# A Strassen step for a part of the second sequence product, with operand sums made beside the scores

## The chip, the cores and the metric

The kernel runs on one NeuronCore of a Trainium2 chip. The time is the device time of one execution in microseconds; a figure for a kernel is the median over its runs. A profile is one further execution, recorded by the hardware profiler. The engines are named as in the profile: PE is TensorE (matrix products), PEld its weight loads, DVE is VectorE, ACT is ScalarE, POOL is GpSimd, SP is SyncE, which here only issues transfers. ScalarE issues transfers too.

## The reference

With x of 2048 positions (S) by 640 features (D), the result is `g * a + (1 - g) * b`, where `g = sigmoid(sum(x * gate_w))` per position.

- Branch a is the real part of a two-dimensional Fourier transform by matrices: `a = Cr @ (x @ Dr.T) - Ci @ (x @ Di.T)`, with Cr and Ci of 2048 by 2048 (the first and second sequence matrix) and Dr and Di of 640 by 640.
- Branch b is a layer of 256 experts with product keys. Each position has 32 heads; each head scores two times 16 keys, takes the best two of each sixteen, adds them to four candidates, keeps the best two and weighs them by a softmax. A chosen expert e contributes `gelu(x . u[e]) * v[e]`.

All of it is in float32.

## The kernel before

**Order of branch a.** The kernel multiplies by the sequence matrices first and keeps the result in DRAM as `pd[w, c]`, with w the matrix (0 for Cr, 1 for Ci) and c one of four chunks of 512 positions. A chunk of a matrix is 16 **pieces** (w, c, s), each a 128x512 block loaded to a tile `wf`. `seq_piece` multiplies one piece by the five 128-wide tiles of x (d = 0 to 4) into five PSUM banks that gather the 16 pieces of a chunk. There are 128 pieces, in the order w, c, s. The **last part** (`step`) multiplies by the 640 by 640 matrices; it is already a Strassen form, in two halves b of 42 steps each, seven units of six steps (a11, a12, s1, s2, s4, s3, a22).

**Products.** A float32 operand is split into a high part (ScalarE, `split`, L123) and a low part (L124, POOL or VectorE). `mm3` makes a product of three matmuls from them (L128 to L130). Pieces are loaded five ahead and split three ahead, into a ring `WS` of four.

**Branch b runs between the pieces.** Work is hung on piece numbers with `at(n, f)` and emitted by `follow(n)` after piece n. Pieces 0 to 30 are beside the preparation of the score weights. Pieces 31 to 70 are the **score stage**: for each of eight pairs p of 128-position tiles, five pieces and four `score_half` calls (five products each), then `u_pair`. ScalarE copies scores from two alternating banks (5 and 6) to tiles `sc`, of which there are two; VectorE takes the top two of each sixteen from them (`topk`), and every four tiles `gates` computes the weights, with one exponential on ScalarE. `rows` then transposes the results by transfers and copies them. After that follows the **expert work** (`experts`): 32 builds of 0/1 matrices on VectorE into four hot buffers (L579 to L581, three operations each), their matmuls (`use`, L607, 32 small ones per build), a copy out of PSUM by ScalarE (L588), and a store to `gd`. Two hot buffers are given up before the last part (L932, L933), because their room becomes a part of the ring there.

**What sets the order.** Each engine executes its instructions in the order in which the program emits them. VectorE work of branch b is emitted by a credit account (`Pump`): each product of TensorE calls `run_bg(0.68)`, which earns 0.68 times a share; while the account is positive, the next piece of work is emitted and its booked price taken off (for a build 3.3, for a `use` 0.2). With nothing to emit, the account is set to 0. Other VectorE work takes its price off the account too (`bg.credit -= ...`). The share is 0.95 before the expert work opens, 1.25 after, 0.95 for the last eight pieces, and in the last part 0.0 for ten steps and then 1.05 (L921, L941). The expert work opens when all 16 tiles' rows are there (L923 and following), which needs p2's pool to be closed. `load_z(b, n)` loads, for the last part, sums of the expert work of half b; before that it emits all expert work still needed for that half (`bg.drain`, L772). For the second half this is hung on step 38 of the first (L914).

**Queues.** SP issues nearly all loads, in order; an issue that must wait for a buffer or for data holds up all behind it. ScalarE issues the stores.

## Time and profile before

| | us |
|---|---|
| median of 3 runs | 773.94 (773.1 to 774.1) |
| the profiled execution's own time | 773.85 |
| its span, first to last instruction | 772.1 |
| TensorE busy | 766.7 |
| VectorE busy | 516.2 |
| POOL busy | 346.5 |
| ScalarE busy | 287.3 |

The span is what the profile's rows divide; the rest of the execution's own time, 1.75 us, lies around it. Matmuls are pipelined, so a row's duration for one is longer than the distance from one to the next. A group's row gives the line, engine, operation, output and inputs, shapes and count, then the busy time and mean of one in ns, then the engine's idle time ahead of the group and what ended it. Rows of one tile or line give the minimum, median and maximum in ns, and the first and last start. Rows of a timeline give the start, the duration and the instruction. Rows of stretches give, for each engine, its busy time and count.

### The profile page before, as it was taken

How to read it: one execution, taken by the hardware profiler on the slowest of the kernel's cores; microseconds unless marked ns; L12 is line 12 of the kernel's file. 1: busy time of each engine (PE TensorE's matmuls, PEld its weight loads, DVE VectorE, ACT ScalarE, POOL GpSimd, SP SyncE). 2: the span in 40 equal slices, each digit the busy share in tenths (PEclk: the TensorE clock that was granted, in tenths of full speed). 3: DMA queues.
4: the chain of work that ended last, by engine and by line, in shares of the span. 5: the costliest groups of instructions: out<-in, count | busy, mean ns of one | idle time of the engine just before them, and what ended most of it. 6: DMA issues, size and time to landing. Idle time of an engine off the chain costs nothing.

```text
span 772.1 us, 11964 instructions
## 1 busy us (share of the span) xinstructions
PE 766.7 (99%) x4616; PEld 620.3 (80%) x4616; DVE 516.2 (67%) x611; ACT 287.3 (37%) x470; POOL 346.5 (45%) x235
## 2 busy tenths in 40 slices
PE   9999999999999999999999999999999999999997
PEld 6777677888888888888888888777788888788886
DVE  7642122276888698579988592677677789747761
ACT  5334324322214432353343462332243453543341
POOL 4522224315143242325242875343446765577253
PEclk9999999999999999999999999999999999999999
DMA  9976985603030440223325454453565586686411
GB/s 343 375 259 191 315 317 191 213 0 117 14 102 25 149 147 15 84 67 130 120 54 169 138 157 122 97 153 89 143 187 169 184 296 218 204 252 220 128 54 70
DMA packets 86953, 121.21 MB, mean 157 GB/s; under 512 B 33136, under 2 KB 40432, under 8 KB 86896
## 3 DMA queue, kind: packets, MB, share of 16 engines
q1 hardware_dynamic: 57360, 100.64, 39.7%
q10 hardware_dynamic: 29536, 19.81, 8.1%
q8 instruction: 36, 0.59, 0.3%
q14 instruction: 21, 0.17, 0.1%
HBM read 98.91 MB, written 19.93 MB: 154 GB/s over the span
## 4 chain that ended last, share of the span: by engine, by line
PE 98%; ACT 1%; POOL 0%; issue 0%; DVE 0%; ACTq 0%; DVEq 0%
PE b L128 31%; PE b L129 31%; PE b L130 31%; PE b L326 2%; PE b L607 1%; PE b L338 1%; PE b L211 1%; PE b L278 0%; POOL WS L124 0%; ACT L396 0%; ACT WS L123 0%; ACT ST L806 0%; ACT wp L332 0%; ACT WP L123 0%; ACT ST L218 0%
## 5 line engine op out<-in xcount | busy, mean ns | idle before, releaser
L124 POOL TENSOR_TENSOR WS<-wf,WS 128x512 fp32r<-128x512 f32 x126 | 189.6, 1509 | 279.3 <-ACT WS L123 250.3
L128 PE MATMUL b<-WS,X 128*128 128x512 f32 x635 | 251.2, 396 | 0.2 <-ACT ST L218 0.2
L129 PE MATMUL b<-WS,X 128*128 128x512 f32 x635 | 247.6, 390 | 0.0
L130 PE MATMUL b<-WS,X 128*128 128x512 f32 x635 | 247.5, 390 | 0.0
L128 PEld LDWEIGHTS b<-WS,X 128*128 128x128 f32 x635 | 119.2, 188 | 33.4 <-issue 7.3
L130 PEld LDWEIGHTS b<-WS,X 128*128 128x128 f32 x635 | 119.2, 188 | 25.4
L129 PEld LDWEIGHTS b<-WS,X 128*128 128x128 f32 x635 | 119.3, 188 | 23.5
L123 ACT ACTIVATE WS<-wf 128x512 fp32r<-128x512 f32 x128 | 80.6, 630 | 113.7 <-PE b L130 57.2
L443 DVE TENSOR_REDUCE mm<-sc 128x64 f32<-128x1024 f32 x32 | 39.0, 1219 | 46.3 <-ACT sc L429 45.7
L124 POOL TENSOR_TENSOR xl<-xf,xh 128x640 fp32r<-128x640 f32 x16 | 33.6, 2123 | 70.4 <-ACT xh L123 64.0
L124 POOL TENSOR_TENSOR WS<-ra,WS 128x512 fp32r<-128x512 f32 x40 | 59.7, 1512 | 12.0 <-ACT WS L123 12.0
L130 PE MATMUL b<-WU,xl 128*128 128x512 f32 x160 | 62.2, 389 | 0.0
L128 PE MATMUL b<-WU,xh 128*128 128x512 f32 x160 | 62.2, 389 | 0.0
L129 PE MATMUL b<-WU,xh 128*128 128x512 f32 x160 | 62.2, 389 | 0.0
L429 ACT ACTIVATE sc<-b 128x512 f32<-128x512 f32 x32 | 21.1, 661 | 100.4 <-PE b L130 93.5
L579 DVE TENSOR_TENSOR hot<-rows,wtab 128x1024 f16<-128x1024 f16 x32 | 30.0, 938 | 36.9 <-PE b L607 36.9
L123 ACT ACTIVATE WS<-ra 128x512 fp32r<-128x512 f32 x56 | 34.8, 630 | 51.8 <-PE b L130 29.8
L124 POOL TENSOR_TENSOR WP<-ra,WP 128x512 fp32r<-128x512 f32 x20 | 32.5, 1636 | 45.2 <-ACT WP L123 45.1
L749 DVE TENSOR_TENSOR ra<-ra 128x512 f32<-128x512 f32 x48 | 45.6, 1002 | 4.2 <-POOL WP L124 4.2
L192 DVE SCALAR_TENSOR_TENSOR ST<-ST,grow 128x512 f32<-128x512 f32 x40 | 37.1, 992 | 15.9 <-DMA grow<-gdr 15.9
L341 DVE TENSOR_TENSOR WU<-b,WU 128x512 fp32r<-128x512 f32 (+1 forms) x16 | 7.8, 490 | 57.2 <-ACT WU L340 57.2
L445 DVE TENSOR_TENSOR eq<-sc,mm 128x1024 f16<-128x1024 f32 x32 | 44.4, 1388 | 1.1
(132 smaller groups left out, 1182.4 us busy)
## 6 DMA issues: line engine op xcount, KB each, us to landing
wq<-in_wq SPq DMA_DIRECT2D x32, 640.0 KB, 6.7
ra<-pd SPq DMA_DIRECT2D x70, 256.0 KB, 3.7
wf<-in_wsim SPq DMA_DIRECT2D x64, 256.0 KB, 2.9
wf<-in_wsre SPq DMA_DIRECT2D x63, 256.0 KB, 5.4
pd<-ST ACTq DMA_DIRECT2D x40, 256.0 KB, 3.1
xf<-in_xT SPq DMA_DIRECT2D x16, 320.0 KB, 3.2
xr<-in_xn SPq DMA_DIRECT2D x15, 320.0 KB, 6.4
out_y<-ST ACTq DMA_DIRECT2D x7, 512.0 KB, 3.8
```

What stands on the lines that cost most here:

```text
L123: nc.scalar.activation(h, f, AF.Copy)
L124: eng.tensor_sub(l, f, h.bitcast(F32))
L128: nc.tensor.matmul(o, wh, ah, start=first, stop=False, skip_group_check=more)
L129: nc.tensor.matmul(o, wh, al, start=False, stop=False, skip_group_check=more)
L130: nc.tensor.matmul(o, wl, ah, start=False, stop=last, skip_group_check=more)
L192: nc.vector.scalar_tensor_tensor(f, f, -1.0 if w else 1.0, g, op0=OP.mult, op1=OP.mult)
L326: nc.tensor.matmul(ps[32 * j:32 * j + 32, :HALF], kp[:, 8 * G // H, r, :], w[:, j], start=(r == 0), stop=(r == 1))
L429: nc.scalar.activation(scs[i].rearrange("p h e -> p (h e)")[:, c], ps, AF.Copy)
L443: nc.vector.tensor_reduce(m, sc, op=OP.max, axis=AX.X)
L445: nc.vector.tensor_tensor(eq, sc, m[:, :, None].to_broadcast([P, HH, E]), op=OP.is_equal)
L579: nc.vector.tensor_tensor(pt, row(0), wt, op=OP.is_equal)
L749: nc.vector.tensor_add(take((b, o, k)) if f is not None else raw[b, o, k], raw[b, o, k] if f is None else f, raw[b, what, k])
```

## The change

The product of the second sequence matrix with x is made in another way for chunks 0 and 1 and the feature tiles d = 0 to 3. The matrix is seen as 2 by 2 blocks: row block r is chunk r, column block the lower or upper eight of the 16 s. x is seen likewise, with the columns of tiles 0, 1 and of tiles 2, 3. Seven block products replace eight (the Winograd form): units a11, a12, s1, s2, s4, s3, a22, each with k = 0 to 7 and two products (`quad_step`). Tile 4 is multiplied along with the units a11, a12, s3 and a22, as a third product. After a11, units stand alternately: s1 with a12, s2 with s4, s3 with a22.

- **Order of pieces.** The first matrix as before (pieces 0 to 63), then chunk 2 of the second matrix (64 to 79), 56 units (80 to 135), and chunk 3 (136 to 151). The last part begins at 152 instead of 128.
- **Left operand sums** (s1 to s4): for each pair p of the score stage, SP loads four blocks of the matrix, VectorE makes four sums of 128x512 and SP stores them to `sd` in DRAM. Two of the four blocks use two of the five `wf` tiles meanwhile.
- **Right operand sums**: for each pair, two halves of x are loaded, VectorE makes four sums of 128x256, and they are stored to `td`. In the units they are loaded again and split, by ScalarE and VectorE.
- **Results**: ScalarE copies some banks, VectorE adds others to them, and the gate is multiplied in, for pairs of tiles; `gate_piece` and `store_piece` aren't used for these two chunks.
- **Account**: the sums take 3.6 and 2.0 per pair, a right-hand split 0.7, a result add 0.7, a gate 0.9. The share stays 0.95 until the units are over.
- **Else**: the expert work opens only when no gate row is loaded; two `wf` tiles are added then; the expert matmuls always use bank 7; the last piece group and the last part use other banks; the last two splits of the 640 by 640 matrices' tiles go to VectorE.

```diff
+HN = NT // 2
+Q0 = 5 * NT
+Q1 = Q0 + 7 * HN
+NPC = Q1 + NT
+QUNITS = [("a11", k) for k in range(HN)] + [(w, k) for ws in (("s1", "a12"), ("s2", "s4"), ("s3", "a22"))
+                                           for k in range(HN) for w in ws]
+TSTEPS = [n for n, (w, k) in enumerate(QUNITS) if w in ("s1", "s2", "s3", "a22")]
...
+    sd = dram.tile([4, HN, P, TC], F32, name="sd")
+    td = dram.tile([HN, P, 4, 2 * P], F32, name="td")
...
-    pieces = [(w, c, s) for w in range(2) for c in range(NC) for s in range(NT)]
+    order = ((0, 0), (0, 1), (0, 2), (0, 3), (1, 2))
+    pieces = [(w, c, s) for w, c in order for s in range(NT)] + [None] * (Q1 - Q0) + [(1, 3, s) for s in range(NT)]
...
-            banks[:] = [bank(d) for d in range(KD)]
-        load_piece(n + 5)
+            banks[:] = [bank(d) for d in ((3, 4, 5, 6, 0) if n >= Q1 else range(KD))]
+        load_piece(n + (7 if p3 else 5))
...
-        for d in range(KD):
+        for d in ((4, 0, 1, 2, 3) if n == NPC - 1 else range(KD)):
...
+    def load_t():
+        j = qs["load"]
+        if j == 0:
+            qs["raw"] = big.tile([P, 5, 2 * P], F32, name="tr", tag="xl")
+        what, k = QUNITS[TSTEPS[j]]
+        nc.sync.dma_start(qs["raw"][:, j % 5], td[k, :, ("s1", "s3", "a22", "s2").index(what)])
+        qs["load"] += 1
+
+    def split_t():
+        j = qs["split"]
+        if j == 0:
+            qs["hl"] = [big.tile([P, 2, 2, 2 * P], F32R, name="tq", tag=t) for t in ("xf", "xh")]
+        tq[Q0 + TSTEPS[j]] = t = [qs["hl"][j % 4 // 2][:, j % 2, a] for a in range(2)]
+        split(qs["raw"][:, j % 5], *t, nc.vector)
+        bg.credit -= 0.7
+        qs["split"] += 1
+
+    for j, t in enumerate(TSTEPS):
+        at(Q0 + TSTEPS[j - 3] - 1 if j >= 3 else Q0 + t - 4 + j, split_t)
+        at(Q0 + TSTEPS[j - 7] - 1 if j >= 7 else Q0 + TSTEPS[0] - 7 + j, load_t)
...
+    def q_add(name, f, a):
+        nc.vector.tensor_tensor(qres[name][:, a], qres[name][:, a], f, op=OP.add)
+        bg.credit -= 0.7
+
+    def q_gate(f, r):
+        nc.vector.scalar_tensor_tensor(f, f, -1.0, grow[NC + r], op0=OP.mult, op1=OP.mult)
+        bg.credit -= 0.9
...
+    def quad_step(n):
+        what, k = unit(n)
...
+        load_piece(n + 7)
+        split_piece(n + 3)
+        h, l = psp.pop(n)
+        o = {"a11": "X", "a12": "Z", "s1": "Y", "s2": "X", "s4": "Y", "s3": "X", "a22": "Z"}[what]
...
+        for d in ds:
+            if d < 2:
+                c = slice(d * P, (d + 1) * P)
+                mm3(qrole[o][d], t[0][:, c], t[1][:, c], h, l, k == 0 and not more, end, more)
+            else:
+                c = slice(4 * P, KD * P)
+                mm3(qrole["W"], wx[:, 0, c], wx[:, 1, c], h, l, k == 0 and low, end and what != "s3", what == "a12")
+            run_bg(0.68)
+        if end:
+            q_post(n, what)
+
+    at(Q0 + 17, load_row, NC)
+    at(Q0 + 45, load_row, NC + 1)
...
+    def sums_load(k):
+        two = [wf_tile("sa") for n in range(2)]
+        tags[:] = [t for f, t in two]
+        t = p2.tile([P, 2, TC], F32, name="sx", tag="sx")
+        for f, r, s in ((two[0][0], 0, 0), (two[1][0], 0, 1), (t[:, 0], 1, 0), (t[:, 1], 1, 1)):
+            sa[r, s] = f
+            nc.sync.dma_start(f, wsim[r, k + HN * s])
+
+    def sums_make(k):
+        a11, a12, a21, a22 = (sa[r, s] for r in range(2) for s in range(2))
+        nc.vector.tensor_add(a21, a21, a22)
+        nc.vector.tensor_sub(a11, a21, a11)
+        nc.vector.tensor_sub(a12, a12, a11)
+        nc.vector.tensor_sub(a22, a11, a22)
+        bg.credit -= 3.6
...
+    def x_make(k):
...
+        nc.vector.tensor_sub(b21, b21, b22)
+        bg.credit -= 2.0
...
+    sums_parts = {0: sums_load, 3: sums_make, 5: sums_store, 6: x_load, 8: x_make, 9: x_store}
...
     for p in range(NP):
         n = N0 + 5 * p
-        for a in range(4):
-            at(n + 1 + a, score_half, 2 * p + a // 2, a % 2)
+        for a in range(5):
+            at(n + a, sums_part, p, 2 * a)
+            if a:
+                at(n + a, score_half, 2 * p + (a - 1) // 2, (a - 1) % 2)
+            at(n + a, sums_part, p, 2 * a + 1)
...
-            t = bank(7, shape) if last_part else ps_s(shape)
+            t = bank(7, shape)
...
-        split(draw[m][:, a], DD[:, w, 0, k], DD[:, w, 1, k], nc.gpsimd)
+        split(draw[m][:, a], DD[:, w, 0, k], DD[:, w, 1, k], nc.vector if m == KD - 1 else nc.gpsimd)
...
-        share = 0.95 if p3 is None or ending else 1.25
-        seq_piece(n)
+        share = 0.95 if p3 is None or ending or n < Q1 else 1.25
+        (quad_step if Q0 <= n < Q1 else seq_piece)(n)
         follow(n)
-        if n >= N1 and p3 is None and len(rowed) == NT and n % NT not in (NT - 2, NT - 1):
+        if n >= N1 and p3 is None and len(rowed) == NT and not grow:
             p2_stack.close()
             p3 = ctx.enter_context(tc.tile_pool(name="p3", bufs=1, reuse_waits="tile"))
             pools.append(p3)
+            wf_tags.extend((p3, f"wf{n}") for n in (5, 6))
```

More of the change, by code (lines that the diff above doesn't have):

```diff
@@ L148, in gated_mix_kernel, with wf_tile, unit, source @@
     gt = const.tile([P, NT], F32)
-    pieces = [(w, c, s) for w in range(2) for c in range(NC) for s in range(NT)]
+    order = ((0, 0), (0, 1), (0, 2), (0, 3), (1, 2))
+    pieces = [(w, c, s) for w, c in order for s in range(NT)] + [None] * (Q1 - Q0) + [(1, 3, s) for s in range(NT)]
     pf, psp, X, xr = {}, {}, {}, {}
-    def load_piece(n):
-        if n < NPC:
-            w, c, s = pieces[n]
-            pf[n] = big.tile([P, TC], F32, name="wf", tag="wf", bufs=5)
-            nc.sync.dma_start(pf[n], (wsre, wsim)[w][c, s])
+    wf_tags = deque((big, f"wf{n}") for n in range(5))
+    def wf_tile(name):
+        pool, tag = wf_tags.popleft()
+        return pool.tile([P, TC], F32, name=name, tag=tag), (pool, tag)
+    def unit(n):
+        return QUNITS[n - Q0]
+    def source(n):
+        if not Q0 <= n < Q1:
+            w, c, s = pieces[n]
+            return (wsre, wsim)[w][c, s]
+        what, k = unit(n)
+        if what[0] == "s":
+            return sd[int(what[1]) - 1, k]
+        return wsim[int(what[1]) - 1, k + HN * (int(what[2]) - 1)]
+    loaded = 0
+    def load_piece(n):
+        nonlocal loaded
+        while loaded <= min(n, NPC - 1):
+            pf[loaded] = wf_tile("wf")
+            nc.sync.dma_start(pf[loaded][0], source(loaded))
+            loaded += 1
     WS = big.tile([P, 4, 2, TC], F32R, name="WS", tag="WS")
@@ L165, in split_piece @@
             psp[n] = WS[:, n % 4, 0], WS[:, n % 4, 1]
-            split(pf.pop(n), *psp[n], eng)
+            f, tag = pf.pop(n)
+            split(f, *psp[n], eng)
+            wf_tags.append(tag)
     then = {}
@@ L216, in seq_piece @@
             if s == NT - 1:
-                staged[n // NT, d] = f = stage()
+                staged[w * NC + c, d] = f = stage()
                 nc.scalar.activation(f, banks[d], AF.Copy)
             run_bg(0.68)
-    for q in range(2 * NC):
-        n = NT * (q + 1)
+    tq, qs = {}, {"load": 0, "split": 0}
+    def load_t():
[5 more added lines that the diff above has]
+        qs["load"] += 1
@@ new lines, in q_out, with w_out, q_post @@
+    def q_out(n, name, o, r, dp):
+        for a in range(2):
+            at(n + a, q_add, name, qrole[o][a], a)
+            at(n + a + 1, q_gate, qres[name][:, a], r)
+        at(n + 6, q_put, name, r, dp)
+    def w_out(r, f):
+        if r == 0:
+            nc.vector.scalar_tensor_tensor(f, qrole["W"], -1.0, grow[NC], op0=OP.mult, op1=OP.mult)
+        else:
+            nc.vector.tensor_tensor(f, f, qrole["W"], op=OP.add)
+            q_gate(f, r)
+        bg.credit -= 0.7
+    def q_post(n, what):
+        if what == "a11":
+            nc.scalar.activation(qres["w"], qrole["W"], AF.Copy)
+            q_copy("c", "X")
+        elif what == "s1":
+            q_copy("c22", "Y")
+        elif what == "a12":
+            f = p3.tile([P, TC], F32, name="wrow")
+            at(n, w_out, 0, f)
+            at(n + 6, lambda: nc.scalar.dma_start(pd[1, 0][4], f))
+            q_out(n, "c", "Z", 0, 0)
+        elif what == "s2":
+            q_copy("c", "X")
+        elif what == "s4":
+            q_out(n + 1, "c", "Y", 0, 1)
+            at(n + 4, grow.pop, NC)
+        elif what == "s3":
+            q_copy("c", "X")
+            for a in range(2):
+                at(n + 2, q_add, "c22", qres["c"][:, a], a)
+                at(n + 3, q_gate, qres["c22"][:, a], 1)
+            at(n + 5, q_put, "c22", 1, 1)
+        else:
+            at(n, w_out, 1, qres["w"])
+            at(n + 2, lambda: nc.scalar.dma_start(pd[1, 1][4], qres["w"]))
+            q_out(n + 2, "c", "Z", 1, 0)
+            at(n + 6, grow.pop, NC + 1)
@@ new lines, in quad_step @@
+    def quad_step(n):
+        what, k = unit(n)
+        if k == 0:
+            if what in ("a11", "s3"):
+                qrole["W"] = bank(0)
+            if what in ("a12", "a22"):
+                qrole["Z"] = [bank(1), bank(2)]
+            if what == "s1":
+                qrole["Y"] = [bank(3), bank(4)]
+            if what == "a11":
+                qrole["X"] = [bank(5), bank(6)]
+        load_piece(n + 7)
+        split_piece(n + 3)
+        h, l = psp.pop(n)
+        o = {"a11": "X", "a12": "Z", "s1": "Y", "s2": "X", "s4": "Y", "s3": "X", "a22": "Z"}[what]
+        low = what in ("a11", "s3")
+        wx = X[k if low else HN + k]
+        if what in ("a11", "a12"):
+            t = [wx[:, a, :2 * P] for a in range(2)]
+        elif what == "s4":
+            t = [wx[:, a, 2 * P:4 * P] for a in range(2)]
+        else:
+            t = tq.pop(n)
+        more = what in ("s2", "s4", "s3")
+        end = k == HN - 1
+        ds = [0, 1]
+        if what not in ("s1", "s2", "s4"):
+            ds = [2] + ds if end or what == "s3" and k == 0 else ds + [2]
+        for d in ds:
+            if d < 2:
+                c = slice(d * P, (d + 1) * P)
+                mm3(qrole[o][d], t[0][:, c], t[1][:, c], h, l, k == 0 and not more, end, more)
+            else:
+                c = slice(4 * P, KD * P)
[3 more added lines that the diff above has]
+            q_post(n, what)
```

42 lines of the change are left out of this document (35 added, 7 removed).

## The prediction

> **What bounds the kernel now.** I read the page's busy times and its chain first, then single matmuls, then stretches of the run for the engines beside the TensorE, and last the expert work (L572 to L613), because the change moves that in time.
>
> ```profile
> span 772.1 us, 11964 instructions
> PE 766.7 (99%) x4616; PEld 620.3 (80%) x4616; DVE 516.2 (67%) x611; ACT 287.3 (37%) x470; POOL 346.5 (45%) x235
> ...
> PE 98%; ACT 1%; POOL 0%; issue 0%; DVE 0%; ACTq 0%; DVEq 0%
> ```
>
> TensorE is busy 99% of the span and is 98% of the chain that ended last. So a removed matmul is worth its full pitch, and any wait put into TensorE's order is paid in full. The pitch, from four matmuls in a row:
>
> ```profile
> 149.73 0.39 PE L128 MATMUL b<-WS,X 128*128 128x512 f32 x1
> ...
> 149.96 0.39 PE L129 MATMUL b<-WS,X 128*128 128x512 f32 x1
> ...
> 150.18 0.39 PE L130 MATMUL b<-WS,X 128*128 128x512 f32 x1
> ...
> 150.41 0.39 PE L128 MATMUL b<-WS,X 128*128 128x512 f32 x1
> ```
>
> One mm3 product (three matmuls) takes 150.41 - 149.73 = 0.68 us, which is also what the program books for it. Now the engines beside it, by stage (scores, expert work, first half of the last part; columns PE, PEld, DVE, ACT, POOL):
>
> ```profile
> 157.00:435.00 278.00, 278.00 (x1340) 234.94 (x1339) 233.83 (x254) 97.57 (x135) 102.93 (x61) 1.00 0.27 86
> 449.00:574.00 125.00, 125.00 (x1520) 100.63 (x1519) 88.02 (x111) 42.82 (x66) 58.15 (x39) 1.00 0.49 134
> ...
> 620.00:694.00 74.00, 73.92 (x324) 60.22 (x323) 55.72 (x59) 32.28 (x56) 49.40 (x31) 1.00 0.74 246
> ```
>
> VectorE has 278 - 233.8 = 44.2 us free in the score stage, 37 in the expert stage and 18 in the first half of the last part. That slack is what the change spends.
>
> **The change, part by part.** *Products.* Two chunks of the second sequence matrix took 2 x 16 x 5 = 160 products. The units take 7 x 8 x 2 = 112 for tiles 0 to 3 and 4 x 8 = 32 for tile 4: 144. Saved: 16 x 0.68 = **-10.9 us**, all of it on TensorE.
>
> *Operand sums in the score stage.* For each of eight k, VectorE gets four 128x512 and four 128x256 operations. Nearest rows, f32 with both inputs in SBUF:
>
> ```profile
> L749 DVE TENSOR_TENSOR ra<-ra 128x512 f32<-128x512 f32 x48 | 45.6, 1002 | 4.2 <-POOL WP L124 4.2
> L696 DVE TENSOR_TENSOR tf<-dt 128x512 f32<-128x512 f32 x6 | 4.1, 678 | 0.0
> L698 DVE TENSOR_TENSOR tf<-tf 128x256 f32<-128x256 f32 x6 | 3.6, 596 | 0.0
> L698 DVE TENSOR_TENSOR tf<-tf x6: 412/412/1512, 573.4 to 609.3; 128x256 f32<-128x256 f32 x6
> ```
>
> That is 4 x 0.68 + 4 x 0.41 = 4.4 us per k at best and 4 x 1.00 + 4 x 0.60 = 6.4 at the means; I take 5.4. The first set falls before the first tile's scores, the other seven need 7 x 5.4 = 38 of the 44 us free: hidden, with 6 to spare (31 to 45, so at worst nothing to spare). When VectorE falls behind, ScalarE is next: it stands behind the gates' exponential, and behind it stand the score copies that free TensorE's two score banks, and the piece splits.
>
> ```profile
> L469 ACT ACTIVATE cc<-cc 128x128 f32<-128x128 f32 x4 | 1.2, 311 | 27.5 <-DVE cc L468 27.5
> SPq L359 <- POOL xl L124: 154.7, 7, 32.1
> ```
>
> ScalarE already stands there 27.5 us in four times without a TensorE gap. SP's queue is blocked up to 32 us behind the xT load, also without one; the change adds 11 transfers per k to SP, two of its waits on VectorE and one on landed stores. The pieces behind them are used three pieces and two score halves later, some 17 us. I price the stage at **+0.5**, bounds 0 and 6 (one such stand past the banks' lead).
>
> *The units' splits.* POOL now splits 56 unit operands where it split 32 pieces.
>
> ```profile
> L124 POOL TENSOR_TENSOR WS<-wf,WS 128x512 fp32r<-128x512 f32 x126 | 189.6, 1509 | 279.3 <-ACT WS L123 250.3
> L124 POOL TENSOR_TENSOR WS<-wf,WS x126: 1279/1320/2323, 9.3 to 607.6; 128x512 fp32r<-128x512 f32 x126
> ```
>
> Where three-product units stand (2.04 us, or 1.70 on average beside s1), 1.51 fits. The 16 units of s2 and s4 last 2 x 0.68 = 1.36 each: POOL needs 16 x 1.51 = 24.2 us against 21.8 of TensorE, or 21.1 at the median. The ring is three units ahead and expert matmuls add time, so between 0 and 2.4 us; I take **+1.0**. The split of the right-hand sums (32 of 128x256 on VectorE) is issued four to seven units before its use, over 5 us; nothing on the path.
>
> *Results.* Adds and gates for two chunks come to some 19 VectorE operations for 10 removed, at the end of each matrix group, with the banks needed again 16 units later. The tightest is X: copied after the last s2, written again one unit (1.36) and one product (0.68) later, against two copies of 0.6: nothing on the path, up to 1 us if ScalarE is late. The renamed banks of the last part change no order.
>
> *The expert work, moved late.* This is where I expect the loss. The page does not show it, but the program's own credit account does, and the account fits the trace of before: it opens the expert work after piece 86 and places the last expert matmuls in piece 114, 14 pieces before the last part.
>
> ```profile
> 478.77 0.61 PE b L607 x61
> ...
> 572.72 1.15 PE b L607 x127
> ```
>
> A pair of builds costs 6.8 credits (3.3 twice and 0.2), so 32 builds cost 109. Before, each 3.4 us piece earned 1.25 x 3.4 = 4.25 and all were out by 574 us. After, with the sums' charges (5.6 per k) the last tile's top-k ends two pieces later, and the rows come out at unit 13 of the 56. From there:
> - units 14 to 55 hold 105 products: 105 x 0.68 x 0.95 = 67.8 earned, of which right-hand splits take 25 x 0.7 = 17.5 and results 8.7; 41.6 stay, 13 builds with one on account;
> - the last chunk's first eight pieces earn 34.0 at 1.25 and lose 6.4 to results and 12 to the sums of the last part: under 5 builds;
> - its last eight earn 25.8 at 0.95 and lose 17: under 3 builds.
>
> So **21 of 32 builds are out when the last part starts**. In its first half, steps 0 to 9 earn nothing (share 0.0, L941); steps 10 to 37 earn 66 products x 0.68 x 1.05 = 47.1, and gate 3.75, z 3.5, adds 18, splits 9.6 and results 4.2, with 6 owed at the start, take 45. So the account stands near nothing when step 38 asks for the second half's z (L914), and L772 drains the expert work there: by the account two builds come out in steps 37 and 38, and nine in one go behind step 38's matmuls. Only two hot buffers are left by then (L933), so VectorE can be two builds ahead of TensorE and no more, and TensorE, which takes its instructions in order, stands in front of the next expert matmuls until each build is done. Before, at the same place VectorE had nothing of this kind:
>
> ```profile
> 684.26 1.28 DVE L810 TENSOR_TENSOR ST<-ST,b 128x512 f32<-128x512 f32 x2 [7.29 <-ACT ST L806]
> ...
> 681.43 0.39 PE L130 MATMUL b<-WS,vs 128*128 128x512 f32 x1
> ...
> 620.21 0.39 PE L128 MATMUL b<-WP,DD 128*128 128x512 f32 x1
> ...
> 453.75 0.68 DVE L579 TENSOR_TENSOR hot<-rows,wtab 128x1024 f16<-128x1024 f16 x1
> 454.35 0.68 DVE L580 TENSOR_TENSOR hot<-rows,wtab 128x1024 f16<-128x1024 f16 x1
> 454.96 0.68 DVE L581 TENSOR_TENSOR hot<-hot,rows 128x1024 f16<-128x1024 f16 x1
> 455.56 0.68 DVE L579 TENSOR_TENSOR hot<-rows,wtab 128x1024 f16<-128x1024 f16 x1
> ...
> L579 DVE TENSOR_TENSOR hot<-rows,wtab 128x1024 f16<-128x1024 f16 x32 | 30.0, 938 | 36.9 <-PE b L607 36.9
> ```
>
> Unhindered, builds follow each other every 455.56 - 453.75 = 1.81 us. The first of the three operations has a mean of 0.94 against 0.68 at best (the other two are near it), so a build beside POOL's splits takes up to some 2.6. VectorE is free 4.1 us after step 35's last matmul starts (685.5 against 681.4) and then has 11 builds: 20 to 28.6 us, so it ends 24 to 33 us after that point. TensorE by then has three steps of 2.04 and 13 expert groups of 0.31 (0.61 for two), 10.1 us. It stands for 14 to 23 us. POOL runs out of splits early in the stand, so I take a value near the low end: **+16.5**.
>
> *After the drain.* Sums, their store and the z loads now run on the path. One store and one load of this kind take:
>
> ```profile
> gd<-cd ACTq DMA_DIRECT2D x16, 128.0 KB, 3.7
> ...
> ra<-gd SPq DMA_DIRECT2D x32, 64.0 KB, 3.0
> ...
> L588 ACT ACTIVATE cd<-b x16: 597/600/604, 479.5 to 574.0; 128x512 f32<-128x512 f32 x16
> L594 ACTq DMA_DIRECT2D gd<-cd x16: 520/634/1373, 486.4 to 575.2; - x16
> ...
> L779 SPq DMA_DIRECT2D ra<-gd x32: 319/424/1363, 612.7 to 697.9; - x32
> ...
> L788 DVE TENSOR_TENSOR ra<-ra x8: 685/1236/1781, 617.8 to 700.1; 128x512 f32<-128x512 f32 x8
> ```
>
> The copy 0.6, the store's issue 0.6 and landing 3.7, four loads' issues 1.7 and landing 3.0, two VectorE operations 2.5 and the split on ScalarE and POOL (about 0.6 and 1.5) come to 14 us; the operand is used eight steps of 2.04 = 16 us later. It fits by 2 us, but the result add of a22 stands behind it on VectorE, and ScalarE's splits behind that add's output transfer. **+1.0**, bounds 0 and 3.
>
> *The clock.* TensorE's first matmuls took 3.59 us for eight, 0.45 each, double the later pitch of 0.227:
>
> ```profile
> 1.17 3.59 PE b L278 x8
> ```
>
> After a stand of this length a restart may cost the same: 8 x 0.22 = 1.8 us. I take **+1.0** of 0 to 1.8. The Trainium skill ("TensorE: Matmul & The Clock Gate", Part 1) says that the array's clock is halved after about 3.4 us with little work and given back after as long a busy time; by it the restart would cost about 1.7 us, an estimate from that page, where no mid-run gap in this trace shows it either way.
>
> *Sum*, on the profiled execution's own 773.85 (span 772.1 and 1.75 around it; the median of the runs is 773.94, 0.1 above): 773.85 - 10.9 + 0.5 + 1.0 + 16.5 + 1.0 + 1.0 = **783.0 us**.
>
> **The rivals.** (A) *No stand.* The expert work ends before step 38 of the last part. Then it is 773.85 - 10.9 + 0.5 + 1.0 = 764.5, with 763 to 768 around it. For it: VectorE has 37 us free in the expert stage and the added work there is some 30. Against: builds are given out by credit and not by free time, and the account is 37 credits short. It decides if eleven more builds come out earlier than I count. (B) *A short stand.* VectorE gets builds out before step 38 because an entry of the account is smaller than I read it; each build less saves 1.8 to 2.6 us; with five in the drain it is 783.0 - 6 x 2 = 771. (C) *VectorE also bounds the score stage.* At the mean prices its 44 us are used up; then the gates' exponential holds ScalarE past the banks' lead of about 5 us, in up to three places, some 6 us: 789 together with the drain. For it: in the profile ScalarE waits 27.5 us at that place already. Against: the credits charge the sums at 5.6, so top-k is given out later too.
>
> **How the numbers follow.** Forecast 0.65, own range 775 to 788; A 0.13; B 0.09; C 0.13. The range takes in C and B and the low end of the unknown costs: 766 to 791 leaves out A's 0.13 and a few hundredths above. About 0.2%, 1.5 us, is what a measurement of this kernel tells from no change. B is spread over 766 to 776, a little over half of it faster: faster 0.18, within 0.2% 0.03, slower 0.79.
>
> **What would show it.** Expert matmuls (L607 of before) in the profile after 650 us, with eleven groups of 32 inside about 25 us near 670 to 695, TensorE idle between them waiting for VectorE's hot builds, and a dip of TensorE's busy tenths there and nowhere else. The steps before it should stand some 10 us earlier than now: the first product of the last part at about 611 instead of 620.2. The score stage should keep TensorE at 99% with VectorE above 95%. I am wrong if the expert matmuls end before the last part (A), if the stand there is under 10 us (B), or if TensorE shows gaps waiting for ScalarE between 150 and 420 us (C).

## The result and the profile after

The changed kernel takes **818.72 us** (817.59 to 820.3, 4 runs) against 773.83 us of the kernel before (773.1 to 774.1, 4 runs), a ratio of 1.0583 with a 95% interval of 1.0562 to 1.0604. Slower was forecast, but by 9 us and not by 45.

The page of the kernel after: span, busy times, and TensorE's and its clock's tenths in 40 slices.

```profile
span 816.3 us, 12411 instructions
...
PE 770.7 (94%) x4568; PEld 616.1 (75%) x4568; DVE 597.7 (73%) x718; ACT 311.6 (38%) x532; POOL 378.6 (46%) x257
...
PE   9999999999999999999999699889989899849997
...
PEclk9999999999999999999999899999998999959999
```

TensorE has 48 matmuls less (4568 against 4616), which are the 16 products saved, and yet is busy 4.0 us longer and idle 45.6 us against 5.4 (a time in which an engine only waits is called a stand here). Its slices are full up to the end of the score stage, 413.52 us here and 413.41 before; from slice 23 on there are holes, and the clock's slices dip with them. What TensorE waited for:

```profile
PE b L814 <- ACT cd L795: 9.8, 5, 3.9
PE b L814 <- DVE hot L788: 8.7, 6, 2.0
PE b L135 <- POOL WS L130: 7.3, 8, 2.4
PE b L134 <- ACT WS L129: 4.5, 2, 3.5
PE b L136 <- DVE tq L130: 3.3, 3, 1.8
```

(Total, times, longest.) The hot builds of the forecast stand in the second row, but they are one of several. By stretches (columns PE, PEld, DVE, ACT, POOL as in the prediction, then clock, DMA share, GB/s): score stage; entry into the units; units; last 16 pieces; last part to the drain; the drain; the rest.

```profile
157.00:435.00 278.00, 278.00 (x1341) 235.01 (x1340) 260.54 (x306) 94.34 (x130) 94.41 (x55) 1.00 0.49 166
437.00:464.00 27.00, 19.30 (x78) 13.95 (x76) 15.10 (x14) 11.93 (x22) 20.94 (x15) 0.98 0.69 205
464.00:570.00 106.00, 98.41 (x705) 76.83 (x706) 83.39 (x80) 54.89 (x101) 79.77 (x53) 0.96 0.66 204
570.00:637.00 67.00, 61.43 (x531) 49.32 (x529) 59.70 (x84) 24.47 (x54) 34.51 (x28) 0.95 0.51 151
637.00:710.00 73.00, 70.17 (x361) 55.60 (x361) 56.53 (x63) 31.94 (x57) 47.46 (x31) 1.00 0.63 203
710.00:730.00 20.00, 5.37 (x355) 4.43 (x355) 18.95 (x31) 4.23 (x11) 1.22 (x1) 0.63 0.18 29
730.00:812.00 82.00, 80.56 (x350) 66.08 (x348) 42.52 (x54) 30.39 (x51) 41.52 (x28) 0.99 0.51 161
```

Stretch less PE busy is the idle time: 0, then 7.7, 7.6, 5.6, 2.8, 14.6 and 1.4 us. Before, the same places had none. The score stage, where the sums went, lost nothing; the drain lost about what was forecast; and 21 us went at the entry, in the units and behind them, where the forecast had 1.

**The drain** stands where the forecast has it. The first operations of two builds in a row on VectorE, and, in a view of TensorE, two groups of expert matmuls with the idle time ahead of each:

```profile
714.09 0.68 DVE L786 TENSOR_TENSOR hot<-rows,wtab 128x1024 f16<-128x1024 f16 x1
...
715.90 0.68 DVE L786 TENSOR_TENSOR hot<-rows,wtab 128x1024 f16<-128x1024 f16 x1
```

```profile
714.22 0.38 PE L814 MATMUL b<-hot 128*32 128x32 f16 x32 [1.43 <-DVE hot L788]
...
718.86 0.41 PE L814 MATMUL b<-hot 128*32 128x32 f16 x32 [2.42 <-ACT cd L795]
```

A build takes 715.90 - 714.09 = 1.81 us, and TensorE stands before each group of 32 matmuls. Eleven L786 operations begin after 637, so 21 of 32 builds were out.

**The clock** falls behind each long stand, here at 609.7 in the last 16 pieces:

```profile
613.60 0.69 PE L814 MATMUL b<-hot 128*32 128x32 f16 x64 [3.86 <-ACT cd L795]
...
615.25 0.63 PE L136 MATMUL b<-WS,X 128*128 128x512 f32 x1
615.67 0.63 PE L134 MATMUL b<-WS,X 128*128 128x512 f32 x1
...
620.33 0.39 PE L134 MATMUL b<-WS,X 128*128 128x512 f32 x1
620.55 0.39 PE L135 MATMUL b<-WS,X 128*128 128x512 f32 x1
```

After 3.86 us without work the pitch is 0.43 us up to 619.5, and then 0.22 again; from 612.93 to 619.76 the granted clock is 0.50, and TensorE is busy 6.16 us of that. So a stand of 4 us costs about 3 us more. TensorE's busy time shows the sum: without the 10.9 us of saved matmuls it would be 766.7 - 10.9 = 755.8; it is 770.7, 14.9 us more for the same work. Up to the last matmul, the granted clock is 0.50 in four stretches (462.75 to 469.58, 520.77 to 524.19, 612.93 to 619.76 and 715.34 to 732.40) that hold 5.12 + 3.42 + 6.16 + 6.58 = 21.3 us of TensorE's busy time; half of it, 10.6 us, is the price of the lower clock. The other 4.3 us come at full clock. A part of them is how rows count: the last and the first matmul around a stand count with 0.39 and 0.50 us in place of a pitch of 0.23. The version with 1.4 credits below, with a granted clock of 1.00 throughout, also has 4.6 us over 755.8. The halving behind such a stand agrees with the rule of the Trainium skill that the prediction cited ("TensorE: Matmul & The Clock Gate", Part 1); the clock came back 6.8 us after it fell, at 619.76. What failed was how often the rule was applied.

### The profile page after: what moved, and what is told of

The parts are those of the page before. It is cut to its first block, busy times and chain, and to the rows that moved or that the text cites. A ratio compares the mean times of both kernels' runs of the same rounds, so it can differ in the third digit from the quotient of the medians.

```text
span 816.3 us, 12411 instructions
## 1 busy us (share of the span) xinstructions
PE 770.7 (94%) x4568; PEld 616.1 (75%) x4568; DVE 597.7 (73%) x718; ACT 311.6 (38%) x532; POOL 378.6 (46%) x257
## 5 line engine op out<-in xcount | busy, mean ns | idle before, releaser
L130 POOL TENSOR_TENSOR WS<-wf,WS 128x512 fp32r<-128x512 f32 x150 | 225.9, 1520 | 247.6 <-ACT WS L129 235.7
L135 PE MATMUL b<-WS,X 128*128 128x512 f32 x555 | 220.0, 396 | 7.6 <-POOL WS L130 7.3
L134 PE MATMUL b<-WS,X 128*128 128x512 f32 x555 | 222.0, 400 | 4.9 <-ACT WS L129 4.5
L136 PE MATMUL b<-WS,X 128*128 128x512 f32 x555 | 218.7, 394 | 0.0
L134 PEld LDWEIGHTS b<-WS,X 128*128 128x128 f32 x555 | 105.5, 190 | 36.8 <-issue 7.8
L135 PEld LDWEIGHTS b<-WS,X 128*128 128x128 f32 x555 | 105.8, 191 | 32.8 <-POOL WS L130 11.1
L129 ACT ACTIVATE WS<-wf 128x512 fp32r<-128x512 f32 x152 | 94.4, 628 | 85.4 <-PE b L136 25.7
L136 PEld LDWEIGHTS b<-WS,X 128*128 128x128 f32 x555 | 105.5, 190 | 22.2
L129 ACT ACTIVATE WS<-ra 128x512 fp32r<-128x512 f32 x56 | 34.9, 630 | 56.2 <-DVE ra L956 26.9
L130 POOL TENSOR_TENSOR WP<-ra,WP 128x512 fp32r<-128x512 f32 x20 | 34.5, 1739 | 43.4 <-ACT WP L129 40.5
L130 DVE TENSOR_TENSOR tq<-tr,tq 128x256 fp32r<-128x256 f32 x32 | 27.5, 875 | 22.6 <-ACT tq L129 22.2
L668 ACT ACTIVATE rows<-rt 128x384 f16<-128x384 f16 x16 | 31.2, 1951 | 33.5 <-DMA rt<-gs 33.5
L956 DVE TENSOR_TENSOR ra<-ra 128x512 f32<-128x512 f32 x48 | 36.3, 804 | 9.2 <-DMA ra<-pd 9.2
```

The source lines that it names most:

```text
L129: nc.scalar.activation(h, f, AF.Copy)
L130: eng.tensor_sub(l, f, h.bitcast(F32))
L134: nc.tensor.matmul(o, wh, ah, start=first, stop=False, skip_group_check=more)
L135: nc.tensor.matmul(o, wh, al, start=False, stop=False, skip_group_check=more)
L136: nc.tensor.matmul(o, wl, ah, start=False, stop=last, skip_group_check=more)
L668: nc.scalar.activation(ROWS[i // 8][:, :, :, i % 8], t, AF.Copy)
```

## The experiments

My first theory, from the trace: the account hands out builds too late (theory 1), and the stand in the drain is the cost. The rivals: VectorE itself is the bound in the units (theory 2); VectorE and GpSimd shut each other out there (theory 3). And the entry into the units has a cause of its own.

All experiments but the last two are single runs, beside which the kernel before took 774.1 to 774.9 us. The last two, with four runs each, spread over 6 us, so a difference of two or three us between single runs shows little by itself; what a run shows is read from its trace.

**More credit in the units.** Only the share of the units is changed.

```diff
-        share = 0.95 if p3 is None or ending or n < Q1 else 1.25
+        share = 0.95 if p3 is None or ending else 1.6 if n < Q1 else 1.25
```

> Changed kernel with the share in the units raised from 0.95 to 1.6, nothing else. By the credit account all 32 builds are then out by the sixth of the last eight pieces, so nothing is left for the drain in the last part. Theory 1 (the late expert work costs what its stand shows: 14.6 us of TensorE idle between 710 and 729 and slow matmuls behind it): the stand goes and the time falls by 18 to 25 us, to about 796; the waits at the entry into the units (437 to 464) stay. Rival (VectorE is the bound from the units on, so the builds only move the stand forward): TensorE waits in the units for the right-hand splits grow by 10 us or more and the time falls by less than 8 us.

814.8 us. The drain is gone, the last part takes 147.9 us (148.0 before), but its first product comes at 660.9 instead of 637.25. TensorE's waits of this kernel:

```profile
PE b L135 <- POOL WS L130: 11.4, 7, 4.1
PE b L136 <- DVE tq L130: 10.2, 5, 3.7
```

The stand has moved into the units: theory 1 alone falls.

**The sums left out.**

```diff
-        nc.vector.tensor_add(a21, a21, a22)
...
-        nc.vector.tensor_sub(b21, b21, b22)
```

> Changed kernel without the eight VectorE operations per k that make the operand sums beside the scores; their transfers and their charges to the account stay, so the order of all else is the same. The sums are left out: the matrix blocks themselves are stored in their place, and the result is not the reference's. Theory 2 (VectorE's lag at the end of the scores holds ScalarE at the last exponential, with it POOL's splits of the 640 by 640 matrices, SP's queue behind them, the late gate row and ScalarE's stores): the 8.2 us of idle between 437 and 464 shrink to under 3 and the time falls by 8 to 14 us, to about 807. Rival (SP's own added transfers and the shorter units cause the entry's stall): the idle there stays above 6 us and the time falls by less than 4 us.

815.94 us, 2.8 below the changed kernel and not the 8 to 14 that I expected. TensorE's idle time between 437 and 464 us falls from 7.7 to 3.5 us, and 2 us of it come back behind the units, between 600 and 637. The sums beside the scores are nearly free, as forecast.

**The gate row earlier, its stores later** (piece row 4, whose stores fall into the first units).

```diff
-        at(n + (2 if q == 0 else -2 if q > 1 else -1), load_row, q)
+        at(n + (2 if q == 0 else -6 if q == 6 else -2 if q > 1 else -1), load_row, q)
...
-        at(n + (8 if q == 0 else 1), store_piece, q)
+        at(n + (8 if q == 0 else 5 if q == 6 else 1), store_piece, q)
```

> Changed kernel with the gate row of the last plain chunk before the units loaded four pieces earlier and its five stores issued four units later, so that ScalarE does not stand in its queue behind the gates on VectorE at the start of the units. If the last link of the entry's chain is that stand (ScalarE's store issues from 454.8 to 460.2), the idle between 458 and 464.5, 5.9 us, and the half-speed matmuls behind it go and the time falls by 6 to 9 us, to about 811. If the wait for pieces that SP loaded late is the real limit, the idle only moves and the time falls by less than 3 us.

817.06 us. The stand of 3.5 us at 458 went, and one of 2.5 us came at 470.6: moving a block in a queue moves the stand.

**The last eleven builds left out.**

```diff
+            if g == 1 and c >= 5:
+                return
```

> Changed kernel in which the VectorE operations of the last eleven builds of the second half are left out; their matmuls read what the hot buffers hold, so the result is not the reference's. All order and all of TensorE's work stay. It prices the drain by itself, with nothing moved forward. Theory 1: TensorE's idle between 710 and 729 shrinks from 14.6 us to what the copies out of one bank leave (under 7 us), and the time falls by 12 to 18 us, to about 804. If the stand has another cause (the sums' store, the z loads), it falls by less than 5 us.

816.64 us, where I expected 804. With no build to wait for, TensorE still stands 10.9 us in the drain, against 14.6 with the builds; another engine is named now:

```profile
715.75 0.38 PE L816 MATMUL b<-hot 128*32 128x32 f16 x32 [0.54 <-ACT cd L797]
719.47 0.41 PE L816 MATMUL b<-hot 128*32 128x32 f16 x32 [3.35 <-ACT cd L797]
```

The stretch of the drain, with no work on VectorE (columns as above):

```profile
710.00:730.00 20.00, 9.10 (x400) 6.63 (x399) 0.00 (x0) 5.79 (x14) 2.54 (x2) 0.67 0.26 42
```

All groups use bank 7, each waits for the copy out of it, and every fourth for the store of `cd`. So the drain has a second floor 3.7 us under the builds, which I had not priced. A faster VectorE would have helped it by no more than that.

**What VectorE and GpSimd do to each other.** Groups of instructions between 470 and 570 us (busy us, mean ns | idle time ahead), of the kernel before, where its builds are:

```profile
L579 DVE TENSOR_TENSOR hot<-rows,wtab 128x1024 f16<-128x1024 f16 x28 | 24.7, 881 | 36.9 <-PE b L607 36.9
L580 DVE TENSOR_TENSOR hot<-rows,wtab 128x1024 f16<-128x1024 f16 x28 | 21.2, 758 | 0.0
L581 DVE TENSOR_TENSOR hot<-hot,rows 128x1024 f16<-128x1024 f16 x28 | 20.1, 718 | 0.0
...
L124 POOL TENSOR_TENSOR WS<-wf,WS 128x512 fp32r<-128x512 f32 x27 | 40.6, 1506 | 60.2 <-ACT WS L123 60.2
```

and of the changed one:

```profile
L130 DVE TENSOR_TENSOR tq<-tr,tq 128x256 fp32r<-128x256 f32 x31 | 26.9, 881 | 21.8 <-ACT tq L129 21.4 <-DMA wf<-sd 0.4
L787 DVE TENSOR_TENSOR hot<-rows,wtab 128x1024 f16<-128x1024 f16 x13 | 18.7, 1438 | 0.0
L788 DVE TENSOR_TENSOR hot<-hot,rows 128x1024 f16<-128x1024 f16 x12 | 18.0, 1504 | 0.0
L786 DVE TENSOR_TENSOR hot<-rows,wtab 128x1024 f16<-128x1024 f16 x13 | 16.5, 1270 | 0.0
...
L130 POOL TENSOR_TENSOR WS<-wf,WS 128x512 fp32r<-128x512 f32 x49 | 74.9, 1554 | 24.7 <-ACT WS L129 22.5 <-PE b L136 2.1
```

With 49 GpSimd splits in place of 27, a build takes 1.27 + 1.44 + 1.50 = 4.2 us instead of 2.36. In order of time (VectorE, then GpSimd):

```profile
520.49 1.76 DVE L786 TENSOR_TENSOR hot<-rows,wtab 128x1024 f16<-128x1024 f16 x1
522.18 1.77 DVE L787 TENSOR_TENSOR hot<-rows,wtab 128x1024 f16<-128x1024 f16 x1
...
529.60 0.68 DVE L786 TENSOR_TENSOR hot<-rows,wtab 128x1024 f16<-128x1024 f16 x1
```

```profile
519.02 9.21 POOL L130 TENSOR_TENSOR WS<-wf,WS 128x512 fp32r<-128x512 f32 x6 [2.49 <-ACT WS L129]
529.82 12.94 POOL L130 TENSOR_TENSOR WS<-wf,WS 128x512 fp32r<-128x512 f32 x8 [1.60 <-ACT WS L129]
```

Beside GpSimd's splits each build operation takes 1.7 us, where it takes 0.68 at 529.60, in GpSimd's pause. That looks like taking turns, one instruction each. It slows GpSimd too: eight splits in a row beside builds take 12.94 us, 1.62 each, where three of them with little work on VectorE (0.8 us in that time) take 1.33 each:

```profile
476.15 3.98 POOL L130 TENSOR_TENSOR WS<-wf,WS 128x512 fp32r<-128x512 f32 x3 [3.07 <-ACT WS L129]
```

The shortest unit lasts 1.36 us, so GpSimd alone would have kept up with it, and beside the builds it does not. Four runs test the theory. First, GpSimd's share left out (the low parts of the unit operands are not made):

```diff
-        split_piece(n + 3)
+        split_piece(n + 3, None if n + 3 < Q1 else nc.gpsimd)
```

> Changed kernel in which POOL does not make the low parts of the unit operands (units 3 to 55): the low parts are left out, the matmuls read what the ring holds, and the result is not the reference's. VectorE's work, the account and TensorE's work are unchanged. In the profile of the changed kernel a build takes 4.2 us between 470 and 570 against 2.4 before, with its operations in step with POOL's. Theory 3 (VectorE operations with two operands in SBUF and POOL's splits exclude each other, so the two engines share one budget that the units overdraw): a build falls to 1.8 to 2.0 us, a right-hand split from 0.88 to about 0.45, the idle of TensorE between 488 and 542 (7 us) falls under 2 and the time by 6 to 12 us, to about 809. Rival (VectorE's own work or its order is the limit): operations keep over 0.7 of their lengths and the time stays within 3 us.

805.37 us. Builds fall to 0.76, 0.69 and 0.69, the right-hand splits from 0.88 to 0.43 us, and TensorE has no wait in the units between 464 and 596. Then with all work done, the same splits on VectorE:

```diff
-        split_piece(n + 3)
+        split_piece(n + 3, nc.vector if n + 3 < Q1 else nc.gpsimd)
```

> Changed kernel with the low parts of the unit operands made by VectorE instead of POOL (53 operations of 128x512, about 0.69 us alone against POOL's 1.28), all computed, no charge. Theory 3: the shared budget falls by 53 x 0.6 = 32 us in the units, builds take about 1.9 us, and the idle in the units goes: 5 to 12 us less, about 809; the drain stays. Rival (VectorE itself has too much to do): 36 us more on it make the units' waits longer, and the time is 5 us or more above the changed kernel.

805.76 us, and in 470 to 570:

```profile
L130 DVE TENSOR_TENSOR WS<-wf,WS 128x512 fp32r<-128x512 f32 x45 | 30.3, 689 | 1.6 <-ACT WS L129 0.9
L130 DVE TENSOR_TENSOR tq<-tr,tq 128x256 fp32r<-128x256 f32 x31 | 13.0, 422 | 14.6 <-ACT tq L129 14.6
L786 DVE TENSOR_TENSOR hot<-rows,wtab 128x1024 f16<-128x1024 f16 x15 | 11.4, 761 | 2.4 <-PE b L814 2.4
```

The other two build groups have 11.4 and 10.3 us, so VectorE does 45 splits more and two builds more in the same stretch in 30.3 + 13.0 + 11.4 + 11.4 + 10.3 = 76.4 us, where splits and builds took 26.9 + 18.7 + 18.0 + 16.5 = 80.1. Work taken from GpSimd onto the fuller engine made the kernel 13 us faster: that is theory 3, and theory 2 in its plain form has no room for it. The Trainium skill ("SBUF — State Buffer", section "SBUF: two separate sides") has this rule: a VectorE operation with both inputs in SBUF and a GpSimd operation that reads SBUF use one pair of ports, and whichever starts first keeps it for its whole instruction while the other stands. The rows agree with it: 0.68 us for a build operation alone, 1.76 and 1.77 beside GpSimd's splits.

Then both kernels with more credit (1.6 without GpSimd's splits; 1.25 with VectorE's):

> The run without POOL's low parts in the units (left out, so the result is not the reference's), and the share in the units raised to 1.6. Theory 3: with POOL out of the way VectorE can take all builds inside the units, so neither the drain's stand nor the units' waits are left: 25 to 35 us less than the changed kernel, about 788, with what stays at the entry into the units. If the share alone moved the stand for another reason than POOL, the middle of the run (score end to last part) stays near the 246 us of the run with the share alone.

780.56 us, 38 below the changed kernel, where 25 to 35 were expected; 28 builds in 470 to 570, no drain, the last part 148.2 us. TensorE still waits 4.4 us for a copy out of bank 7, at 603 to 607.

> The run with VectorE's splits in the units and the share there 1.25: the account then has 27 builds out at the last part and some 4 for the drain. Theory 3: the drain shrinks from 18 to some 7 us while the units hold, about 797. Rival: the units lose what the drain gains, within 4 us of the run with VectorE's splits alone.

798.14 us; the drain shrinks to 700.97 to 709.8 with 7.5 us idle. So theory 1 is right as a second condition: once the two engines don't shut each other out, credit does move the builds ahead.

**Can the gain be had?** Three kernels with VectorE splits, 1.6 credits, the expert groups on banks 1 and 2 in the pieces after the units, the last top-k rows given out sooner, and row 4's gate earlier with its stores later; the second moves the `DD` splits later and to VectorE, the third gives all pieces' splits to VectorE too.

```diff
-            t = bank(7, shape)
+            t = bank(7 if last_part or here[0] < Q1 + 4 else 1 + rotate("use", 2), shape)
...
-            at(N1 + 3 + 2 * m + a, split_dd, m, a)
-        at(N1 + 4 + 2 * m, load_dd, m + 3)
+            at(N1 + 6 + m, split_dd, m, a)
+        at(N1 + 6 + m, load_dd, m + 3)
```

> The changed kernel with five edits: low parts of the unit splits on VectorE, 1.6 credits per microsecond in the units, the expert groups of the first pieces after the units on banks 1 and 2 in turn instead of bank 7 alone, the last rows of the top-k given out at a spacing of 8 and 4 instead of 16 and 5, and the gate load of piece row 4 earlier with its stores later. All work is done. If the time lost is the shared budget of VectorE and GpSimd in the units plus the builds left for the drain, there is no stand behind step 38 (last part 148 us, as before's), the first product of the last part comes at 627 or earlier, and the time is 774 to 782. If instead the drain comes back because VectorE, which now also splits, can't give out 32 builds in the units, the last part takes 155 us or more and the time is 785 to 798. By the one-bank reading the 4 us stand of TensorE behind the copy of an expert sum near 600 us is gone.

> The same, and the splits of the unit operands of s1 and s2 (DD) come later, one per piece, with their low parts on VectorE alone. All work is done. If the entry into the units stands (4 us of TensorE idle at 440 to 465) because those splits fall into the piece in which VectorE is late and GpSimd then blocks the draw loads, that idle is gone and the time is 3 to 5 us below the run without this edit. If the entry stands because VectorE is overbooked in the score stage, the idle stays or grows, by up to 8 x 0.69 = 5.5 us of added VectorE work.

> The same again, and from the first unit on every split, the pieces' too, has its low part on VectorE, so that GpSimd has no operation on these tiles in units and last part. All work is done. If the budget that VectorE and GpSimd share is what counts, the 0.69 us of a VectorE split against 1.5 us on GpSimd makes the last part no longer than 148 us and the whole some 2 us shorter at most. If in the last part the two ran beside each other without harm, VectorE is 56 x 0.69 = 39 us fuller there and the last part is longer by up to 20 us.

792.15, 795.29 and 789.92 us: slower than I expected (774 to 782 for the first, and the second below the first). None has a drain (last part 148 us each); the one bank's stand of 4 us near 600 is gone in the first two, and the third waits 1.9 us at 579. Most of what is left sits at the entry. TensorE's gaps of the third at 452 to 476, and ScalarE's rows there:

```profile
454.80 0.60 PE L134 MATMUL b<-WS,X 128*128 128x512 f32 x1 [2.75 <-ACT WS L129]
...
475.91 0.80 PE L134 MATMUL b<-WS,X 128*128 128x512 f32 x1 [5.36 <-ACT WS L129]
```

```profile
436.67 0.31 ACT L628 ACTIVATE cc<-cc 128x128 f32<-128x128 f32 x1 [8.51 <-DVE cc L627]
...
468.68 6.43 ACTq L231 DMA_DIRECT2D pd<-ST  x5
475.23 1.15 ACT L129 ACTIVATE WS<-wf 128x512 fp32r<-128x512 f32 x2 [4.63 <-DMA pd<-ST]
```

Two queues are blocked. ScalarE stands 8.5 us for the late top-k, so `DD`'s splits are late and SP stands at a `draw` load from 429 to 445, with the units' loads behind it. And five stores hold ScalarE for 6.4 us. It is not the issuing: one issue takes 0.33 to 0.45 us, and between the third (over at 470.42) and the fourth nothing is issued for 3.9 us.

```profile
474.30 0.81 ACTq L231 DMA_DIRECT2D pd<-ST  x2
```

```profile
469.21 0.38 SPq L188 DMA_DIRECT2D wf<-sd  x1
```

In the trace's semaphore records the fourth store waits for the semaphore that this load of SP uses as well, and the last part of the load lands at 473.78. So the store stands for a transfer of another queue. Before had such a block too, 4.72 us for four stores from 450.19 on (the third of its five, at 453.17, stands for a load of SP that landed at 453.10), without any harm.

There a piece lasts 3.4 us and splits are three ahead, a lead of 10 us; three units of 1.36 to 2.04 us are a lead of 4 to 6. So the entry was cleared: `DD` is split from the tiles that `make_sums` loads anyway in the last 16 pieces, and row 4's stores go out one per unit.

```diff
+            for j, d in enumerate((4, 2, 3, 0, 1)):
+                at(n + 1 + j, store_one, q, d)
...
+        if k < KD:
+            at(NPC - 14 + 2 * k, split_dd, k)
```

> As the run with all splits on VectorE from the first unit on, but the splits of the unit operands DD of the last part are taken from the tiles that make_sums loads anyway, in the last 16 pieces, so that the ten draw loads and ten splits at the entry into the units are gone, and the five stores of piece row 4 are issued one per unit instead of five in a row. All work is done. If TensorE's idle of 9.7 us at 452 to 476 comes from SP blocked at the draw loads (429 to 445) and from ScalarE blocked at five stores in a row (6.4 us), it is gone, with some 5 us of half clock behind it: the first product of the last part at about 621, and 774 to 777 us. If it comes from the top-k that VectorE ends late, idle of 5 us or more stays there and the time stays above 784.

> The same with 1.4 credits per microsecond in the units instead of 1.6: some 20 us x 0.2 x 3 = 12 credits less, 3 to 4 builds later. All work is done. If VectorE is still the tight engine inside the units, the waits of TensorE for VectorE's splits there (2.6 us at 514 and 536 in the run before) shrink and the time is 1 to 4 us lower than with 1.6. If not, the time is the same or, with builds back in the last part, higher.

778.29 and 777.49 us, beside 774.85 for the kernel before on that chip; 774 to 777 was expected of the first. The long gaps at 452 to 476 are gone, and what is left there is under 1 us each, though in the first the clock still falls for 3.4 us at 471; the two edits were not run apart. In the second the clock is 1.00, the first product of the last part comes at 620.30, and the longest waits from 415 on are 1.8 us, right ahead of that product, and 1.1 us behind it. Its 205 us from 415 to 620 hold 199.60 us of TensorE work, where before had 206.80 without a gap: 7.2 of the 10.9 us show as less work, 5.4 are given back as idle, 2.9 in the last part (150.9 against 148.0), and 1.6 ahead of all this, where the score stage ends at 415.0. Last, two kernels with four runs each, with row 4's stores two per unit and row 7's one per step (the first with 1.5 credits and half of `DD`'s low parts on GpSimd; the second with 1.6 and the pieces' low parts on GpSimd):

> As the run with the entry cleared, with 1.5 credits per microsecond, the stores of piece row 4 two per unit (so that they have landed before the copies of the first units' results), those of row 7 one per step, and the second half of the DD splits on GpSimd. All work is done. If what is left is queue order alone, TensorE's idle falls from 9 to some 6 us and the time is 771 to 775. If VectorE's amount of work in the units is what is left, idle of 3 us or more behind VectorE's splits stays there and the time is 775 to 779.

> The same store order with 1.6 credits, the low parts of the pieces after the units on GpSimd again (as in the changed kernel), and the DD splits on VectorE. All work is done. By then the builds are out, so GpSimd and VectorE meet less there; if so, the time is within 2 us of the run beside it. If the two still shut each other out in the last 16 pieces, where the sums of the last part run on VectorE, there are waits of TensorE for GpSimd's splits after 570 and the time is 3 us or more higher.

781.86 us (779.48 to 785.42), ratio 1.0104 with an interval of 1.0072 to 1.0136; and 787.78 us, 1.0167 (1.0136 to 1.0198). The first is above what I expected (771 to 779), and the second 5.9 us above the first. In the first, waits behind VectorE's splits stay (2.3 and 1.6 us in all), so its amount of work in the units counts and not queue order alone; the second waits 2.0 us for a GpSimd split at 569, where the builds end and the sums of the last part begin. None of the versions beats the kernel before. That the change cannot gain is not shown by this; a version that gives the units less VectorE work was not tried.

## Why the prediction was right in sign and wrong in size

The terms of its sum, against the trace after (from the stretches and busy times above):

| term | forecast | measured |
|---|---|---|
| products saved | -10.9 | 48 matmuls less, 48 x 0.227 = -10.9 |
| operand sums in the score stage | +0.5 | +0.1 |
| entry, units and last 16 pieces (POOL's splits) | +1.0 | +20.9 idle |
| last part up to the drain | 0 | +2.8 idle |
| the drain's stand | +16.5 | +14.6 idle |
| after the drain | +1.0 | +1.4 idle |
| clock | +1.0 | +10.6 busy |
| busy time added at full clock | no term | +4.3 busy |
| sum | +9.1 | +43.8 (spans: 816.3 - 772.1 = +44.2) |

*Products* and *operand sums*: right; what the sums cost at the entry is at most the 2.8 us of the run without them. VectorE is busy 260.54 of 278 us in the score stage (93.7%, a little under the 95% forecast) and TensorE 278 of 278. Rival C, the same bound in that stage, did not happen there: ScalarE did stand at the exponential (8.2 us, to 434), but its price fell due behind the stage, at the entry.

*The units' splits*: **this step failed.** It set 16 x 1.51 = 24.2 us of GpSimd against 21.8 of TensorE and took VectorE's time as separate: "VectorE has ... 37 [us free] in the expert stage". The two slacks are one. The mean build of 2.36 us before, against 1.81 at best, was the sign; I used it as a price of at most 2.6 us per build in the drain, and not as a budget that 22 more splits would overdraw. From 413.5 to 637.2 TensorE needed 223.7 us for what would be 206.8 - 10.9 = 195.9, 28 us more; without GpSimd in the units the first product of the last part comes at 624.9, with VectorE's splits at 626.5, so 11 to 12 of the 28 are this, the slow clock behind it included. GpSimd's 1.51 us in that sum was itself a mean taken beside VectorE's work; with little beside it a split takes 1.33, as the forecast's own median of 1.32 says, and that is under the 1.36 of the shortest unit.

The rest of the 28 had no term in the sum. One part is the entry (7.7 us idle and a half clock behind it): a lead counted in units is about half as long in us as one in pieces. The other is the stand of 3.86 us in the last 16 pieces, with its half clock: a copy out of bank 7 stood in ScalarE's order behind splits that had waited 3.79 us for VectorE's sums of the last part:

```profile
609.78 1.28 ACT L129 ACTIVATE ts<-tf 128x256 fp32r<-128x256 f32 x3 [3.79 <-DVE tf L903]
```

*The expert work*: right in its count (21 of 32 out, eleven left), its place (step 38's drain, 710 to 730) and its pace (1.81 us a build). Its size (14.6 idle of a forecast 14 to 23) is right in part by luck: with no builds at all TensorE stands 10.9 us there, for bank 7 and `cd`, so the builds alone set only the last 3.7 us. The first product of the last part was forecast at 611 and came at 637.25.

*After the drain*: right, 1.4 us.

*The clock*: right in kind (half pitch for some 6 us of work after the stand at 610), wrong in number. It was counted once; there were stands at 458, 519, 610 and all through the drain, where bursts of 32 small matmuls every 1.8 us left the granted clock at 0.63 and it did not recover until 732.

*Rivals A and B* rested on the builds coming out earlier. The kernel with more credit had no drain at all and still took 814.8 us, so A would not have given its 764.5.

## What to carry to other kernels

Before moving work onto a free VectorE or GpSimd, add up the time of VectorE's operations with two SBUF inputs and of GpSimd's in that stretch: they share one budget, and a mean well above the minimum of one shape is the first sign that it is being used up. When a loop's step gets shorter, recount every lead in microseconds, since a queue block that was covered by three long steps is not covered by three short ones. When TensorE is the bound and runs without gaps, price a new stand at more than its length where a slow clock follows: one of 3.86 us cost some 3 us more here, a single one of 1.8 us nothing.

## What the runs showed of the hardware that I had not expected

The clock also fell without one long stand: after two waits of 0.98 and 0.85 us in a row, with a single matmul between them, at 519 to 520 of the changed kernel the pitch went to 0.43 us for 3 us:

```profile
518.99 0.50 PE L134 MATMUL b<-WS,X 128*128 128x512 f32 x1 [0.98 <-ACT WS L129]
520.34 0.50 PE L135 MATMUL b<-WS,X 128*128 128x512 f32 x1 [0.85 <-POOL WS L130]
```

```profile
517.36:520.77 3.41, 1.58 (x6) 0.76 (x5) 2.23 (x5) 2.46 (x6) 1.75 (x2) 1.00 0.93 318
520.77:524.19 3.42, 3.42 (x10) 2.67 (x9) 3.42 (x3) 0.97 (x3) 3.42 (x3) 0.50 0.97 350
```

Other gaps of that length left it alone (the version with 1.4 credits has one of 1.8 us and a mean clock of 1.00). The traces show what decides. In all that have any, a mid-run stretch of half clock lasts a whole number of 3.41 us windows, and the stretches of one run lie on one grid of such windows. On that grid, over all 17 traces from 10 us on, at full clock all 34 windows in which TensorE was busy less than 0.43 of the time were followed by half clock, 10 of the 31 between 0.43 and 0.6, and none of the 3706 above. At half clock all 42 windows busy over 0.95 were followed by full clock, 2 of the 4 between 0.86 and 0.95, and none of the 47 below. The window above was busy 1.58 of 3.41 us, 0.46. So in these runs it is the share of work in one window that counts, and not the length of one stand, and a gap can do harm or none by where it falls on the grid.
